# Sparse attention and routed experts on one core: v loaded by one DMA per pair, the last batch transposed by DMA, first weights in quarters

## The chip, the cores and the metric

The kernel runs on one core of one Trainium2 chip, as a single program. Its time is measured on the device, in microseconds (us); the median of nine runs is compared. The profile shows one execution, recorded by the hardware profiler, with its own time and span.

A core has a matrix engine (TensorE, PE in the profile; PEld is its loading of weights), a vector engine (DVE), a scalar engine (ACT), a general engine (POOL, GpSimd) and a queue engine (SP). POOL, SP and ACT also issue DMAs, which the core's 16 DMA engines carry out.

## What is computed

Two stages, one after the other. The first is attention over 4 batches, 8 heads, 768 positions and 64 dimensions, in which each position sees its neighbours nearer than 16 and, besides, a summary of each block of 32 positions:

```python
k_sum = k.reshape(B, H, nb, block, D).max(axis=3)
v_sum = v.reshape(B, H, nb, block, D).mean(axis=3)
scores_l_m = np.where(mask_l, scale * q @ k.T, -1e9)       # |i - j| < 16
scores_s   = scale * q @ k_sum.T + np.log(block)
a = softmax(concatenate([scores_l_m, scores_s]))
attn = a @ concatenate([v, v_sum])
```

Its output, as x with 3072 rows and 512 columns, goes to eight experts, which all work on all rows. Their shares P are found from the logits by eight rounds of normalizing rows and columns (the Sinkhorn rounds):

```python
P = exp(x @ w_gate)
for _ in range(8):
    P /= P.sum(1); P /= P.sum(0); P *= N / E
out = sum(P[:, e] * (relu(x @ w1[e]) @ w2[e]) for e in range(8))
```

## The kernel before

**Pairs and batches.** Heads are worked on two at a time: 16 pairs, four to a batch. Pairs 0 to 3 are done in halves of 384 positions (`pair_half`), pairs 4 to 15 whole (`pair_whole`). For one pair, q and k are loaded by POOL (`load_qk`), turned so that the head dimension lies on partitions (`tr` on TensorE through PSUM, copied out by `tr_out`, line 202, on DVE or ACT), keys are maximized by blocks (`key_max`, lines 315 and 318), scores are formed (`score_mms`, line 324; summaries, line 422), exponentiated on ACT, masked on DVE (`masks`, `edges`), multiplied with v (`values`, lines 410 and 416), normalized on DVE (lines 500 and 501), and turned again into xT (`to_xT`, line 508, with `x_out`). v comes by two DMAs a pair, one per head (`load_v`, line 270). A whole pair also needs the neighbours of each 128-row chunk, which four small SBUF-to-SBUF DMAs on SP put into the tile `Ve` (`near_values`, lines 352 and 354). Sums of v by blocks are line 332.

**Experts.** Expert 0 runs inside this stage in eight halves of 384 rows, two per batch (`expert0`): 32 matmuls of 384 columns (line 206) and 24 of 512 (line 211) each. When the last batch's x is there, its logits (line 528) and the Sinkhorn rounds follow (lines 537 to 551). After it the loop over experts 1 to 7 runs, with 64 matmuls of 512 columns for each of six blocks of rows, and the loads of the next expert (lines 187 and 193). DVE adds each result to `out_acc` (line 867) and SP stores it (line 871).

**What sets the order.** In the first stage the order on every engine is written out by a planner, `Plan.order`, before the kernel is built. Each step is a unit with an engine, a cost in us, its predecessors and a priority. The planner picks the unit that can start first by these costs. The engines then follow that order strictly, so an instruction whose input is late holds up all behind it on its engine. Expert 0 has the lowest priority and fills gaps. Where the planner sees TensorE idle before the first relu, it adds matmuls on a tile of zeros (`keep_busy`, line 570).

**DMA queues.** All loads stand in one chain on POOL (`load`). POOL's DMAs share eight semaphores in turn, so that a DMA waits until the eighth before it has landed. The two loads of expert 1's weights come at the end of the chain, behind `transposed`, two one-element copies on POOL that read kT and qT of pair 12.

Transposing by DMA exists in the code (`tr_dma`, `x_dma`, both issued by SP) but the bounds `BY_DMA = 16` and `X_BY_DMA = 16` keep it out of use: there are only pairs 0 to 15. The planner's own costs for one transposing DMA are 1.4 us on SP (1.5 for x), then 1.7 us, then a lag of 2.0 us.

Of the kernel before, what the change touches and what calls it, by code (L numbers as in the profile page):

```python
# [9 lines left out]
FP32 = mybir.dt.float32  # L10
BF16 = mybir.dt.bfloat16
# [101 lines left out]
def kernel(  # L113
# [10 lines left out]
    nc = tc.nc  # L124
# [18 lines left out]
    NEH = 3  # L143
    BY_DMA = 16
    X_BY_DMA = 16
    WHOLE = 12
# [12 lines left out]
    col_en = const.tile([128, 128], FP32)  # L159
    warm = const.tile([1, 8], FP32)  # L160
    zeros = const.tile([128, 512], BF16)
# [46 lines left out]

    def project_mm(e, yp, h, c, fs):
        for f in fs:  # L210
            nc.tensor.matmul(yp[:], lhsT=h[:, f, c * 128:(c + 1) * 128],  # L211
                             rhs=w2s[e][:, f, :], start=(f == 0), stop=(f == KF - 1))

# [6 lines left out]
    with tc.tile_pool(name="attn", bufs=1) as attn, \  # L220
# [7 lines left out]
        ksT = [attn.tile([128, 128], BF16, name=f"ksT{i}") for i in range(NB)]  # L228
        v_x = [attn.tile([128, G, 2, VD], BF16, name=f"vx{i}") for i in range(NQ)]

# [36 lines left out]
        def load_v(i):  # L267
            b, h0 = i // PB, (i % PB) * 2
            for j in range(2):
                nc.gpsimd.dma_start(out=v_x[i % NQ][:, :, j, 0:D],  # L270
                                    in_=v[b, h0 + j].rearrange("(g p) d -> p g d", p=128))

# [55 lines left out]
        def block_sums(i):  # L328
            sv = v_x[i % NQ]
            vs = at["vs", i] = bank("a", "vs")[:, 0:2 * D]  # L330
            for g in range(G):
                nc.tensor.matmul(vs.rearrange("p (j d) -> p j d", j=2), lhsT=m_blk[:, g, :],  # L332
                                 rhs=sv[:, g, :, 0:D], start=(g == 0), stop=(g == G - 1))

# [11 lines left out]
        def near_values(i):  # L346

            sv, ve = v_x[i % NQ], V_e[i % NE]
            eng = nc.sync if i < BY_DMA else nc.gpsimd
            for j in range(2):  # L350
                c0, q0 = VD * j, 64 + 32 * j
                eng.dma_start(out=ve[q0 + W:q0 + 2 * W, 1:G, c0:c0 + VD],
                              in_=sv[128 - W:128, 0:G - 1, j, :])
                eng.dma_start(out=ve[q0:q0 + W, 0:G - 1, c0:c0 + VD],
                              in_=sv[0:W, 1:G, j, :])

# [47 lines left out]
        def values(i, h):  # L404
            sv, ee, ve, em = v_x[i % NQ], E_e[i % NE], V_e[i % NE], at["em", i]
            av = at["av", i, h] = bank("a", "av")
            for cc in range(HG):
                c, o = HG * h + cc, cc * 2 * VD
                for j in range(2):
                    nc.tensor.matmul(av[:, o + j * VD:o + (j + 1) * VD],  # L410
                                     lhsT=em[:, j, c, :], rhs=sv[:, c, j, :],
                                     start=(cc == 0 and j == 0), stop=False,
                                     skip_group_check=True)
            for cc in range(HG):
                c, o = HG * h + cc, cc * 2 * VD
                nc.tensor.matmul(av[:, o:o + 2 * VD], lhsT=ee[:, c, :], rhs=ve[:, c, :],
                                 start=False, stop=True, skip_group_check=True)
# [46 lines left out]
        def values_h(i, h):  # L464
            sv, em, es = v_x[i % NQ], E_h[(PB * h + i) % NEH], at.pop(("es", i, h))
            av = at["av", i, h] = bank("a", "av")

            def mm(p0, p1, cc, j, lhsT, rhs, n=VD, start=False, stop=False):
                o = cc * 2 * VD + j * VD
                nc.tensor.matmul(av[p0:p1, o:o + n], lhsT=lhsT, rhs=rhs, start=start, stop=stop,  # L470
                                 skip_group_check=True)

            for cc in range(HG):
                for j in range(2):
                    mm(0, 128, cc, j, em[:, j, cc, 2 * W:2 * W + 128], sv[:, HG * h + cc, j, :],
                       start=(cc == 0 and j == 0))
            for cc in range(HG):
                c = HG * h + cc
                for j in range(2):
                    if c + 1 < G:  # L480
                        mm(96, 128, cc, j, em[0:32, j, cc + 1, 0:32], sv[0:32, c + 1, j, :])
                    if c > 0:
                        mm(0, 32, cc, j, em[96:128, j, cc - 1 if cc else HG, LIVE:PADL],
                           sv[96:128, c - 1, j, :])
            for cc in range(HG):
                mm(0, 128, cc, 0, es[:, cc, :], V_s[i][:], n=2 * VD, stop=True)
# [129 lines left out]

        def late_constants():
            for t in E_e:
                nc.vector.memset(t[64:128, :, :], 0.0)
            for t in V_e:  # L620
                nc.vector.memset(t[:], 0.0)
                nc.vector.memset(t[0:24, :, D:VD], 32.0)
                nc.vector.memset(t[32:56, :, VD + D:2 * VD], 32.0)
            nc.vector.memset(col_en, float(E) / float(N))

# [9 lines left out]
        def load_pair(i, parts="kqv"):  # L635
            old = i - NQ
            for c in parts:
                if c == "v":
                    load(("v", i), lambda: load_v(i), 1.65, 1.75,
                         [U.get(("A", old, 1)), U.get(("near", old))])  # L640
                elif i < PB and c in "qr":
                    h = "qr".index(c)
                    load(("q", i, h), lambda h=h: load_qk(i, 1, h), 0.65, 0.6)
                else:
                    z = "kq".index(c)
                    load((c, i), lambda z=z: load_qk(i, z), 0.75 if i < PB else 1.65,
                         1.1 if i < PB else 1.55, [U.get(("tr", old, z)), U.get(("tr", old, 2))])

        def pair_start(i, prio):
# [9 lines left out]
            for z in range(0 if i >= BY_DMA else 1 if i < PB else 2):  # L659
# [9 lines left out]
            U["vs", i] = add("PE", 0.4, lambda: block_sums(i),  # L669
                             [U["v", i]] + ([U.get(("A", i - NE, 1))] if i >= PB else []), prio + 0.01, opens=[buf])  # L670
            U["Vs", i] = add("DVE", 0.22 if i < PB else 0.7, lambda: block_out(i), [U["vs", i]],
# [35 lines left out]
        def pair_whole(i, prio):  # L707
            U["near", i] = add("SP" if i < BY_DMA else "POOL", 2.4 if i < BY_DMA else 3.0, lambda: near_values(i),
                               [U["v", i], U.get(("A", i - NE, 1))], prio, lag=3.5)
            x1 = []  # L710
# [14 lines left out]
            for h in range(2):  # L725
                U["mk", i, h] = add("DVE", 0.56, lambda h=h: masks(i, h),
                                    [U["X", i, h], *x1[:h], U.get(("A", i - 2, 1))], prio)
            U["ed", i] = add("DVE", 0.78, lambda: edges(i),
                             [U["X", i, 0], U["X", i, 1], U["mk", i, 1], U.get(("A", i - NE, 1))], prio)
            for h in range(2):  # L730
# [22 lines left out]
        def expert0(t0, xs):  # L753
            key, n = t0, len(halves)
            halves.append(key)
            pr = 1000.0 + n
            w = [U["w1", 0], U["w1", 1]]
            evac, old = [], [U.get(("pj", halves[n - 2], c)) for c in range(HG)] if n >= 2 else []
            for f in range(KF):
                buf = Buffer("m")  # L760

                def fn(f=f):
                    at["hp", key, f] = hidden0(key, t0, f)
                m = add("PE", 0.67, fn, xs + [w[f // 4]] + old, pr + f * 0.01, opens=[buf])

# [30 lines left out]
        load_pair(3, "v")  # L796
        load(("w1", 0), lambda: load_w1(0, 0, 2), 0.85, 2.5)
        for i in range(PB):
            load_pair(i, "r")
        load(("w1", 1), lambda: load_w1(0, 1, 2), 0.85, 2.5)  # L800
        load("w2", lambda: load_w2(0), 0.85, 5.0)
        add("DVE", 4.0, constants, [], -5.0)
        for i in range(PB):
            pair_start(i, i)
            pair_half(i, 0, i)
        add("DVE", 1.8, late_constants, [U["A", PB - 1, 0]], 5.5)
        expert0(0, [U["x", i, 0] for i in range(PB)])
# [14 lines left out]
        def transposed():  # L822

            r = (NP - 4) % NB
            nc.gpsimd.tensor_copy(out=warm[:, 0:1], in_=kT[r][0:1, 0:1])
            nc.gpsimd.tensor_copy(out=warm[:, 1:2], in_=qT[r][0:1, W:W + 1])

        last[0] = add("POOL", 0.3, transposed, [last[0]] + [U["kT", NP - 4, z] for z in range(2)])
        load("w1n", lambda: load_w1(1), 0.85, 5.0)
# [28 lines left out]
    def step2(e, n):  # L858
        h = hs.pop((e, n))
        for c in range(4):  # L860
            t = 4 * n + c
            if e == 1:
                nc.vector.tensor_scalar_mul(out=out_acc[:, t, :], in0=out_acc[:, t, :],
                                            scalar1=P_sb[:, t, 0:1])
            yp = mps.tile([128, 512], FP32, tag="m", name="yps")
            project_mm(e, yp, h, c, range(KF))
            nc.vector.scalar_tensor_tensor(out=out_acc[:, t, :], in0=yp[:],  # L867
                                           scalar=P_sb[:, t, e:e + 1], in1=out_acc[:, t, :],
                                           op0=ALU.mult, op1=ALU.add)
            if e == E - 1:  # L870
                nc.sync.dma_start(out=out[t * 128:(t + 1) * 128, :], in_=out_acc[:, t, :])

# [35 lines left out]
```

The softmax here doesn't subtract the row's maximum and nothing guards it: scores larger than these inputs give would overflow.

## Time and profile before

| | us |
|---|---|
| median of nine runs | 744.05 |
| lowest and highest of them | 743.80, 746.33 |
| the profiled execution's own time | 745.99 |
| its span in the profile | 744.3 |
| start of expert 1's matmuls in the trace | 159.79 |
| TensorE busy | 730.8 (98%) |
| DVE busy | 373.6 (50%) |
| ACT busy | 201.6 (27%) |
| POOL busy | 90.8 (12%) |

Of the nine runs five lie between 743.80 and 744.05 and four between 745.86 and 746.33; the profiled one belongs to the four.

A line of the profile names the line of the code, the engine, the operation, the tile written and the tiles read (buffer numbers left out), and then how often it ran, how long it was busy and how long its engine stood idle just before it. Matmuls are pipelined, so the busy time shown for one is longer than the spacing between two: a matmul of 512 columns is shown with 379 ns, yet 32 of them start within 6.91 us, one every 0.216 us. Where this text speaks of a pace, it is the spacing of starts. A row of windows shows, for a stretch of time, the busy time of each engine, the TensorE clock granted (1.00 is full), the mean number of busy DMA engines as a share of 16, and the bytes moved.

### The profile page before, as it was taken

The page shows a single profiled execution, that of the slowest core. Times are in us where ns is not written, and L with a number is a line of the kernel's source. Part 1 is how long each engine was busy: PE and PEld are TensorE (multiplying, and loading weights), DVE is VectorE, ACT ScalarE, POOL GpSimd, SP SyncE. Part 2 cuts the span into 40 slices and gives each one's busy share as a digit, 9 for nine tenths or more (in the row PEclk, how much of TensorE's full clock was granted, in tenths as well). Part 3 has the DMA queues.
Part 4 walks back from the last instruction along what each step waited for, and adds up shares of the span by engine and source line. Part 5 has one row for each costly group of instructions (what it writes and reads, how often), then busy time and mean ns, then how long its engine had stood idle before and what let it go on. Part 6 is the DMA issues. An engine that isn't in the chain of part 4 may idle for free.

```text
span 744.3 us, 10242 instructions
## 1 busy us (share of the span) xinstructions
PE 730.8 (98%) x4292; PEld 358.8 (48%) x4364; DVE 373.6 (50%) x734; ACT 201.6 (27%) x343; POOL 90.8 (12%) x118
## 2 busy tenths in 40 slices
PE   7999999999999999999999999999999999999997
PEld 4566666554444444444444444444444444444443
DVE  6789976684444444444444444444444444444443
ACT  4577776442112112112112111111121121121120
POOL 8599700010000000000000000000000000000000
PEclk9999999999999999999999999999999999999999
DMA  9999970051003300123003300212003300001212
GB/s 122 164 129 129 107 119 4 1 84 29 1 1 57 57 1 0 22 38 55 1 1 56 58 1 0 41 27 47 1 1 56 57 1 0 1 1 61 95 71 113
DMA packets 86669, 33.68 MB, mean 45 GB/s; under 512 B 68704, under 2 KB 79968, under 8 KB 86624
## 3 DMA queue, kind: packets, MB, share of 16 engines
q0 software_dynamic: 78032, 26.22, 32.9%
q1 hardware_dynamic: 8064, 6.80, 2.9%
q8 instruction: 34, 0.56, 0.3%
q14 instruction: 11, 0.09, 0.0%
q10 hardware_dynamic: 528, 0.02, 0.0%
HBM read 52.45 MB, written 6.29 MB: 79 GB/s over the span
## 4 chain that ended last, share of the span: by engine, by line
PE 93%; DVE 5%; issue 1%; ACT 0%
PE hps L206 44%; PE yps L211 43%; PE idle L570 1%; DVE xs L501 1%; DVE ks L315 1%; PE sg L324 1%; PE av L470 1%; PE tkq L283 1%; PE tx L508 1%; PE ss L422 1%; DVE em L387 1%; PE vs L332 1%; DVE qT L202 0%; DVE kT L202 0%; DVE Ve L342 0%
## 5 line engine op out<-in xcount | busy, mean ns | idle before, releaser
L206 PE MATMUL hps<-xT,w 128*128 128x512 bf16 (+1 forms) x1574 | 343.3, 370 | 1.4
L211 PE MATMUL yps<-w,h 128*128 128x512 bf16 x1493 | 339.5, 379 | 2.2
L197 ACT ACTIVATE h<-hps 128x512 bf16<-128x512 f32 (+1 forms) x220 | 126.1, 573 | 478.5 <-PE hps L206 461.6
L206 PEld LDWEIGHTS <-w 128*128 128x128 bf16 x1600 | 155.1, 98 | 171.8
L211 PEld LDWEIGHTS <-h 128*128 128x128 bf16 x1536 | 149.9, 98 | 175.6
L867 DVE SCALAR_TENSOR_TENSOR out_acc<-yps,P_sb,out_acc 128x512 f32<-128x512 f32 x168 | 126.1, 751 | 166.4 <-PE yps L211 158.5
L199 DVE TENSOR_SCALAR h<-hps 128x512 bf16<-128x512 f32 (+1 forms) x180 | 122.9, 683 | 169.7 <-PE hps L206 169.4
L187 POOL DMA_DIRECT2D w<-in_moe_w_dram x9 | 7.0, 779 | 372.2 <-PE hps L206 371.8
L270 POOL DMA_DIRECT2D vx<-in_v_dram x32 | 29.4, 1023 | 0.0
L383 ACT ACTIVATE er<-sg 128x960 bf16<-128x960 f32 (+1 forms) x28 | 23.5, 857 | 7.5 <-PE sg L324 3.7
L264 POOL DMA_DIRECT2D kst<-in_k_dram x24 | 22.4, 1048 | 7.5 <-DMA w<-in_moe_w_dram 7.5
L264 POOL DMA_DIRECT2D qst<-in_q_dram x24 | 22.5, 1061 | 0.4 <-DMA qst<-in_q_dram 0.4
L193 POOL DMA_DIRECT2D w<-in_moe_w_dram x8 | 9.0, 1121 | 104.2 <-PE yps L211 104.1
L501 DVE TENSOR_TENSOR xs<-av,rc 128x384 bf16<-128x384 f32 x32 | 17.8, 558 | 1.1
L202 ACT COPY out_acc<-yps 128x512 f32<-128x512 f32 x21 | 12.3, 587 | 17.4 <-PE yps L211 16.9
L315 DVE TENSOR_REDUCE ks<-kT 128x24 bf16<-128x768 bf16 x16 | 15.1, 946 | 0.3
L387 DVE TENSOR_TENSOR em<-er,band 128x768 bf16<-128x768 bf16 x24 | 12.8, 548 | 0.6 <-ACT er L383 0.5
L324 PE MATMUL sg<-qT,kT 64*128 64x160 bf16 x208 | 11.8, 230 | 0.2
L432 ACT ACTIVATE Ee<-ss 64x384 bf16<-64x384 f32 x24 | 11.3, 480 | 1.7 <-PE ss L422 1.6
L422 PE MATMUL ss<-qT,ksT 128*128 128x384 bf16 x32 | 9.9, 330 | 1.0 <-DVE ksT L318 0.8
L570 PE MATMUL idle<-zeros 128*128 128x512 bf16 x25 | 9.3, 498 | 1.5 <-DVE vx L576 1.3
L508 PE MATMUL tx<-ident,xs 128*128 128x128 bf16 x96 | 8.9, 221 | 1.3 <-DVE xs L501 1.2
(92 smaller groups left out, 245.1 us busy)
## 6 DMA issues: line engine op xcount, KB each, us to landing
w<-in_moe_w_dram POOLq DMA_DIRECT2D x15, 1024.0 KB, 8.6
out_dram<-out_acc SPq DMA_DIRECT2D x24, 256.0 KB, 2.0
qst<-in_q_dram POOLq DMA_DIRECT2D x32, 96.0 KB, 4.4
vx<-in_v_dram POOLq DMA_DIRECT2D x32, 96.0 KB, 4.7
kst<-in_k_dram POOLq DMA_DIRECT2D x24, 96.0 KB, 4.5
w<-in_moe_w_dram POOLq DMA_DIRECT2D x2, 512.0 KB, 9.2
kst<-in_k_dram POOLq DMA_DIRECT2D x4, 192.0 KB, 5.1
Ve<-vx SPq DMA_DIRECT2D x48, 10.2 KB, 3.7
```

What stands on the lines that cost most here:

```text
L197: nc.scalar.activation(out=out, in_=in_, func=AF.Relu, bias=0.0, scale=1.0)
L199: nc.vector.tensor_scalar_max(out=out, in0=in_, scalar1=0.0)
L206: nc.tensor.matmul(hp[:, 0:n], lhsT=w1s[e][:, dk, f * 128:(f + 1) * 128], rhs=xT[:, dk, t0:t0 + n], start=(dk == 0), stop=(dk == KD - 1))
L211: nc.tensor.matmul(yp[:], lhsT=h[:, f, c * 128:(c + 1) * 128], rhs=w2s[e][:, f, :], start=(f == 0), stop=(f == KF - 1))
L264: nc.gpsimd.dma_start(out=t[:, :, j, :], in_=src[b, h0 + j].rearrange("(g p) d -> p g d", p=128))
L270: nc.gpsimd.dma_start(out=v_x[i % NQ][:, :, j, 0:D], in_=v[b, h0 + j].rearrange("(g p) d -> p g d", p=128))
L315: nc.vector.tensor_reduce(out=ks[i % 2][:, 0, 0:24], in_=kT[r][:].rearrange("p (n w) -> p n w", w=32), axis=AX.X, op=ALU.max)
L324: nc.tensor.matmul(dst, lhsT=kT[r][p0:p0 + 64, g * 128:(g + 1) * 128], rhs=qT[r][p0:p0 + 64, g * 128 + l0:g * 128 + l1], start=True, stop= ...
L383: nc.scalar.activation(out=dst, in_=src, func=AF.Exp, bias=0.0, scale=SCALE)
L387: nc.vector.tensor_tensor(out=at["em", i][:, :, c, :], in0=at["er", i][:, :, c, W:W + 128], in1=band[:, None, None, W:W + 128].to_broadcas ...
L501: nc.vector.tensor_tensor(out=t.rearrange("p g j d -> p (g j) d"), in0=av[:, :, 0:D], in1=rc[:].to_broadcast([128, G, D]), op=ALU.mult)
L867: nc.vector.scalar_tensor_tensor(out=out_acc[:, t, :], in0=yp[:], scalar=P_sb[:, t, e:e + 1], in1=out_acc[:, t, :], op0=ALU.mult, op1=ALU.add)
```

## The change

Six things change together.

- v of a pair comes by one DMA over both heads in place of two. The tile `vx` has its dimensions swapped for it, and every reader of v is re-indexed.
- `BY_DMA` and `X_BY_DMA` go from 16 to 12: for pairs 12 to 15, q and k are turned by `tr_dma` on SP, and x of pairs 12 to 14 by `x_dma` on SP. x of pair 15 stays on TensorE. By the same bound, `near_values` of pairs 12 to 15 moves from SP to POOL, behind all loads.
- `transposed` now waits for the last pair: it reads kT and qT of pair 15 and two corners of its `Ve`, and its unit follows the near rows of pair 15. So expert 1's weights are loaded behind these.
- w1 of expert 0 comes in four DMAs, two before the second halves of q and two after, and each hidden matmul waits for its own quarter.
- The constants of `late_constants` (1.8 us on DVE in one piece) are cut into four units.
- The last projection of expert 7 is done in two halves of 256 columns, each with its own addition and its own store, the second one issued by ACT.

The planner writes a new order with these units. In it 96 transposes of k and q (line 283) stand on TensorE where there were 144, 78 of x (line 508) where there were 96, and 22 matmuls on zeros where there were 28.

```diff
-    BY_DMA = 16
-    X_BY_DMA = 16
+    BY_DMA = 12
+    X_BY_DMA = 12
...
-        v_x = [attn.tile([128, G, 2, VD], BF16, name=f"vx{i}") for i in range(NQ)]
+        v_x = [attn.tile([128, 2, G, VD], BF16, name=f"vx{i}") for i in range(NQ)]
...
-            for j in range(2):
-                nc.gpsimd.dma_start(out=v_x[i % NQ][:, :, j, 0:D],
-                                    in_=v[b, h0 + j].rearrange("(g p) d -> p g d", p=128))
+            nc.gpsimd.dma_start(
+                out=v_x[i % NQ][:].rearrange("p j g x -> p (j g) x")[:, :, 0:D],
+                in_=v[b, h0:h0 + 2].rearrange("j (g p) d -> p (j g) d", p=128))
...
-                    load(("v", i), lambda: load_v(i), 1.65, 1.75,
+                    load(("v", i), lambda: load_v(i), 0.95, 1.75,
...
-            w = [U["w1", 0], U["w1", 1]]
+            w = [U["w1", n] for n in range(4)]
...
-                m = add("PE", 0.67, fn, xs + [w[f // 4]] + old, pr + f * 0.01, opens=[buf])
+                m = add("PE", 0.67, fn, xs + [w[f // 2]] + old, pr + f * 0.01, opens=[buf])
...
-        load(("w1", 0), lambda: load_w1(0, 0, 2), 0.85, 2.5)
-        for i in range(PB):
-            load_pair(i, "r")
-        load(("w1", 1), lambda: load_w1(0, 1, 2), 0.85, 2.5)
+        for n in range(4):
+            load(("w1", n), lambda n=n: load_w1(0, n, 4), 0.85, 1.25)
+            if n == 1:
+                for i in range(PB):
+                    load_pair(i, "r")
...
-        add("DVE", 1.8, late_constants, [U["A", PB - 1, 0]], 5.5)
+        for n in range(NE):
+            U["ec", n] = add("DVE", 0.42, lambda n=n: edge_constants(n), [U["A", PB - 1, 0]], 15 + n)
+            U["vc", n] = add("DVE", 0.5, lambda n=n: value_constants(n), [U["A", PB - 1, 0]], 15.5 + n)
...
-            r = (NP - 4) % NB
-            nc.gpsimd.tensor_copy(out=warm[:, 0:1], in_=kT[r][0:1, 0:1])
-            nc.gpsimd.tensor_copy(out=warm[:, 1:2], in_=qT[r][0:1, W:W + 1])
-
-        last[0] = add("POOL", 0.3, transposed, [last[0]] + [U["kT", NP - 4, z] for z in range(2)])
+            r = (NP - 1) % NB
+            nc.gpsimd.tensor_copy(out=warm[:, 0:1], in_=kT[r][0:32, 0:1])
+            nc.gpsimd.tensor_copy(out=warm[:, 1:2], in_=qT[r][0:32, W:W + 1])
+            ve = V_e[(NP - 1) % NE]
+            for j in range(2):
+                nc.gpsimd.tensor_copy(out=warm[:, 2 + j:3 + j],
+                                      in_=ve[64 + 32 * j:96 + 32 * j, G - 2, VD * j:VD * j + 1])
+
+        last[0] = add("POOL", 0.3, transposed, [last[0], U["near", NP - 1]] + [U["kT", NP - 1, z] for z in range(2)])
...
-            yp = mps.tile([128, 512], FP32, tag="m", name="yps")
-            project_mm(e, yp, h, c, range(KF))
...
-            if e == E - 1:
-                nc.sync.dma_start(out=out[t * 128:(t + 1) * 128, :], in_=out_acc[:, t, :])
+            parts = 2 if (e, t) == (E - 1, NT - 1) else 1
+            for d0 in range(0, DM, DM // parts):
+                d = slice(d0, d0 + DM // parts)
+                yp = mps.tile([128, 512], FP32, tag="m", name="yps")
+                project_mm(e, yp, h, c, range(KF), d)
+                nc.vector.scalar_tensor_tensor(out=out_acc[:, t, d], in0=yp[:, d],
+                                               scalar=P_sb[:, t, e:e + 1], in1=out_acc[:, t, d],
+                                               op0=ALU.mult, op1=ALU.add)
+                if e == E - 1:
+                    (nc.scalar if d0 else nc.sync).dma_start(out=out[t * 128:(t + 1) * 128, d],
+                                                             in_=out_acc[:, t, d])
```

The functions that the change uses in the last batch and did not before are `tr_dma` (one `dma_start_transpose` of a whole tile of 128x768 two-byte elements, 192 KB) and `x_dma` (the same for x); both stand in the printed functions.

## The prediction

> **What bounds the kernel now.** I read the page first, then busy time by stage, then the chain that ended last, then the matrix engine in order of time, then the DMAs.
>
> ```profile
> PE 730.8 (98%) x4292; PEld 358.8 (48%) x4364; DVE 373.6 (50%) x734; ACT 201.6 (27%) x343; POOL 90.8 (12%) x118
> ```
>
> The share 98% is an average. By stage (columns: stretch, its length, PE, PEld, DVE, ACT and POOL busy with counts, clock, DMA share, GB/s):
>
> ```profile
> 0.00:32.00 32.00, 26.79 (x370) 15.46 (x373) 22.02 (x111) 16.44 (x27) 23.59 (x37) 0.95 1.35 148
> 32.00:96.00 64.00, 63.36 (x765) 42.50 (x771) 57.95 (x153) 46.79 (x78) 55.34 (x69) 1.00 1.82 118
> 96.00:160.00 64.00, 63.34 (x530) 38.01 (x535) 47.08 (x125) 37.26 (x72) 0.88 (x1) 1.00 0.25 41
> 160.00:744.30 584.30, 577.27 (x2634) 262.84 (x2686) 246.59 (x348) 101.08 (x169) 10.95 (x11) 1.00 0.16 32
> ```
>
> Only the first 32 us have gaps on PE. From 32 us on PE is full, with DVE 91% busy beside it until 96. The chain in order of time (start, us, what) says that the end is PE alone:
>
> ```profile
> 155.04 4.91 PE yps L211 x22
> 159.95 5.83 PE hps L206 x27
> ...
> 740.15 0.75 DVE out_acc L867
> ```
>
> From 159.79 to 740.12 stand 2688 matmuls of 512 columns at 0.216 us, with no hole. So the change can only move the start of expert 1 (159.79) and the 4.2 us behind the last matmul. The pace of small matmuls is read from starts on PE:
>
> ```profile
> 57.41 0.50 PE L283 MATMUL tkq<-ident,kst 128*128 128x128 bf16 x6
> 57.74 0.50 PE L283 MATMUL tkq<-ident,qst 128*128 128x128 bf16 x6
> 58.08 0.51 PE L332 MATMUL vs<-vx,m_blk 128*128 128x128 bf16 x6
> ```
>
> Six transposes take 0.33 us of PE, 0.055 each, whatever the 220 ns shown for one. Paces of the other kinds: 0.162 for 384 columns, 0.04 for a score, 0.03 to 0.06 for values. Adding them up along the written order gives 26.9 us at the first transposes of pair 4 (trace: 37.27), 83.0 at pair 12's scores (97.31) and 143.8 at expert 1 (159.79). The lag is 10.4, then 14.3, then 16.0: most of what PE loses, it loses before pair 4. In the changed order the same sums are 25.6, 80.7 and 138.9.
>
> **1. Before pair 4** (v in one DMA, w1 in quarters, six idle matmuls less). One v load has 1536 pieces. POOL rows: 0.81 us for 768 pieces, 0.77 for 512 (w1) and 0.89 for 1024 (w2), so about 1.0 against 1.62 for two; bounds 0.8 and 1.62. That is 0.6 us of POOL per pair, 2.5 before w1. But the DMAs behind POOL are late already. Issues at 20.7 to 23.6 (KB each, median us to landing):
>
> ```profile
> w<-in_moe_w_dram POOLq DMA_DIRECT2D x1, 1024.0 KB, 13.6
> kst<-in_k_dram POOLq DMA_DIRECT2D x2, 96.0 KB, 12.8
> ```
>
> The same kind of load lands 4.2 us after issue at 34.4, so here some 8 us are queueing. Pair 4's k landed at 34.6 and 35.2, with the same bytes ahead of it in the changed kernel. PE came to it at 37.27; with 1.3 us of idle matmuls gone and earlier inputs of pairs 1 to 3 it gets there by about 35, and then waits for the landing. I take 35.2: **-2.1**, bounds 0 (the DMAs decide all) and -3.5 (k lands 1.4 earlier). From pair 5 on POOL's saved time is hidden: PE turns pair 12's k at 91, and it was issued at 68. The constants cut in pieces leave DVE free between 26.2 and 28.7, where they held a mask and PE by 0.4; that too is inside the bound.
>
> The clock bears on this part (columns as above):
>
> ```profile
> 14.00:16.00 2.00, 0.91 (x14) 0.60 (x14) 2.00 (x6) 1.14 (x2) 1.65 (x3) 1.00 2.14 155
> 18.00:20.00 2.00, 1.69 (x16) 1.06 (x18) 2.00 (x4) 1.35 (x3) 1.48 (x3) 0.67 1.26 185
> 20.00:22.00 2.00, 1.78 (x11) 0.77 (x8) 1.08 (x5) 1.00 (x1) 1.59 (x2) 0.50 1.29 177
> ```
>
> PE idled half of 14 to 16, and from 18.7 to about 22.1 ran at half clock, 1.7 us of matmul time; most of it covers waiting for pair 3's v. Escaping it is inside the bound of -3.5. [...]
>
> **2. Transposes off PE.** 48 of k and q and 18 of x, 66 x 0.055 = **-3.6**, all in the stretch where PE is full. The weight loads beside them cost nothing (PEld is 66% busy there). The 11 copies out of PSUM that go as well (nine on DVE at 0.55, two on ACT at 0.8) are not on the path.
>
> **3. DVE.** The changed order packs pairs 4 to 15 into 74 us of PE work where it took 83, and moves one whole half of expert 0 behind pair 15. DVE's durations there sum to 73 us against 78. So DVE is as tight as in 32 to 96, but all the way. There the lag grew 3.9 us per 56; later 1.7 per 61. I take **+0.7**, bounds 0 and 2.
>
> **4. The wait for transposed tiles.** The trace has no transposing DMA. Nearest rows: an SBUF-to-SBUF near row, SP 0.58 us and 3.7 to landing, below; a 96 KB load beside weights, 12.8, above. SP is otherwise idle, and the planner's own 1.4 and 3.7 lie near the lower row; I take them. k and q have room: pair 15's may start after pair 12's scores (sum 81, so about 94 us) and its summaries stand at 106, which leaves 10.4 us for issue and landing once key max (1.2) is off; pair 13 has 10.7 (from 79.3, behind pair 11's near rows on SP, to 90), pair 14 more. Pair 12's stand ahead of pair 11's near rows on SP but may start at 72, when those still wait for pair 9's values (77). Needed: 2.8 + 3.7 = 6.5. Nothing is lost. x of pair 14 has less: its values end at 115.5, normalizing takes 1.3, SP 1.4, so it leaves at about 118, and the logits behind it stand at 123.7, with 19 us of expert 0 queued behind them on PE. It shares the DMAs with expert 1's weights, which leave at about 112.5: pair 13's values end at 105, POOL then issues pair 15's near rows (4 x 0.6 to 0.8), these land, and POOL's copies release the loads. Issues at 90 to 95, near rows beside weights:
>
> ```profile
> w<-in_moe_w_dram POOLq DMA_DIRECT2D x2, 1024.0 KB, 10.6
> Ve<-vx SPq DMA_DIRECT2D x3, 10.2 KB, 7.0
> ```
>
> With 7.0 it lands at 125.0: **+1.3**, bounds 0 (3.7) and 7 (12.8). [...]
>
> The weights themselves leave 19.5 us later than before (93.0), land by 123 and are needed at 156: hidden, with 33 us of cover. The near rows of pairs 12 to 15, now on POOL, follow its last load (about 84) or the values of two pairs before (pair 14's 100, pair 15's 105) and are needed 12 us and more later; a POOL load of 96 KB lands within 4.7. The Sinkhorn rounds are covered by the half of expert 0 moved there.
>
> **5. The end.** DVE at 384 and 512 columns of one kind takes 553 and 692 ns, 1.09 a column, so the last addition falls from 0.75 to 0.47; the store of 128 KB lies between 2.0 us (256 KB) and 1.8 (16 KB). **-0.4**, bounds 0 and -0.8. Sixteen matmuls of 256 columns take what eight of 512 did.
>
> **Sum:** -2.1 - 3.6 + 0.7 + 1.3 - 0.4 = -4.1, expert 1 starting at about 156. The profiled execution took 745.99 (span 744.3 and 1.7 around it) and would take 741.9. It belongs to the upper group of runs; from the median 744.05 the forecast is **740.0**.
>
> **Rivals.**
> - *No early gain.* For: POOL waits for the eighth DMA before, and with quarters w2 becomes the eighth after w1's first quarter, so it can leave only when that has landed, about 22 in place of 19.87. If the DMAs run dry meanwhile, w2 and pair 4's k come as late as now. Against: the other quarters and q are still queued (w1's second half landed at 28.5). Time: 742.1.
> - *x late.* The logits wait 5 to 7 us for pair 14's x behind two weight loads of 1 MB. For: the 12.8 above. Against: those were queued behind the loads on POOL; this is on SP. Time: 743.7 to 745.7, called no change.
> - *Slower: a pair's transposes take over 13.4 us from SP to landing.* Then pair 13's summaries wait (L - 10.7) and, since that shifts pair 12's scores, pair 15's wait again (L - 10.4); at 13.4 the two make up for the 4.1 and 1.5 more. At the upper row, 2.8 + 12.8 = 15.6, this is 4.9 + 5.2 = 10, and the time 750. The order is fixed, so the spare half of expert 0 can't fill it. For: nothing of this kind is in the trace, and POOL's loads keep the DMAs busy until pair 15's are in. Against: near rows land in 3.7 us in that very stretch.
>
> That v in one DMA takes POOL as long as two (1.62) is part of the first rival.
>
> **Numbers.** Forecast 0.53 (736.2 to 741.3: early part and end at their best and nothing lost, or DVE at 2), no early gain 0.15, x late 0.14, slower 0.18. What a measurement of this kernel can tell from no change is about 0.2%, 1.5 us. Faster 0.53 + 0.13 = 0.66 (the first rival can come to rest within 1.5 us); same 0.16; slower 0.18. The range goes from 736.2 to 745.5 and leaves the slower case out.
>
> **What would show it.** Expert 1 starts near 156; 66 transposes less; pair 4's k waits for its DMA near 35; a wait of about 1 us before the logits of batch 3, on DMA, with expert 1's weights in flight; the summaries of pairs 13 and 15 without a wait; the last addition near 0.47. I am wrong if a transposing DMA takes over 7 us, if PE shows more than 2 us of waits on DVE between 36 and 110, or if the first 30 us don't shorten.

## The result and the profile after

The changed kernel takes 738.94 us (median of 10 runs, 738.52 to 741.63) against 744.22 for the kernel before, now over 32 runs. The ratio is 0.9931, with a 95% interval from 0.9921 to 0.9940: 5.3 us less, where 4.1 were forecast. The profiled execution took 739.49, with a span of 737.7.

Of the 45 runs of the kernel before whose mean granted clock is known, 11 show 0.998 or less and take 745.07 to 746.59 (median 745.98), while the other 34 take 743.72 to 744.77 (median 744.24), and the profiled execution of before (0.996) is one of the kind of the 11.

The first line of the page of the changed kernel, and busy time by stage (columns as in the prediction):

```profile
PE 724.8 (98%) x4230; PEld 354.7 (48%) x4300; DVE 368.9 (50%) x728; ACT 198.6 (27%) x339; POOL 95.9 (13%) x122
```

```profile
0.00:32.00 32.00, 27.60 (x409) 16.80 (x413) 24.58 (x118) 18.58 (x30) 23.00 (x36) 1.00 1.39 151
32.00:96.00 64.00, 62.40 (x758) 41.56 (x762) 56.59 (x150) 47.33 (x81) 49.66 (x61) 1.00 2.07 139
96.00:160.00 64.00, 63.28 (x455) 35.38 (x462) 47.28 (x128) 34.00 (x65) 15.04 (x16) 1.00 0.31 50
160.00:737.70 577.70, 571.49 (x2615) 260.93 (x2667) 240.47 (x335) 98.67 (x165) 8.20 (x10) 1.00 0.16 33
```

PE is still the bound. The stretch from 32 to 96 shows 1.6 us without PE where before showed 0.6 (a few matmul records are missing: 758 stand beside 762 weight loads, before 765 beside 771). Two starts on PE cut the run into three parts (start, busy time, then the line):

```profile
33.76 0.50 PE L283 MATMUL tkq<-ident,kst 128*128 128x128 bf16 x6
...
153.94 6.42 PE L206 MATMUL hps<-xT,w 128*128 128x512 bf16 x28
```

| | before, profiled | changed, profiled | difference |
|---|---|---|---|
| start to pair 4's first transposes | 37.27 | 33.76 | -3.51 |
| from there to expert 1 | 122.52 | 120.18 | -2.34 |
| expert 1 to the end of the span | 584.51 | 583.76 | -0.75 |
| span | 744.3 | 737.7 | -6.6 |

The first part of these two executions can't be compared as it stands. The same clock windows as in the prediction, now of the changed kernel, show full clock throughout:

```profile
14.00:16.00 2.00, 1.75 (x48) 1.34 (x45) 1.97 (x6) 1.69 (x2) 1.59 (x3) 1.00 2.31 146
18.00:20.00 2.00, 1.76 (x31) 1.19 (x29) 1.48 (x5) 0.56 (x2) 1.22 (x2) 1.00 1.41 196
20.00:22.00 2.00, 1.81 (x29) 1.12 (x28) 1.55 (x5) 0.48 (x1) 0.89 (x1) 1.00 1.45 188
```

The kernel e4 below has before's order up to the end, and its execution kept the full clock. There pair 4 starts at 35.13:

```profile
35.13 0.50 PE L283 MATMUL tkq<-ident,kst 128*128 128x128 bf16 x6
```

So 2.1 of the 3.51 us lie between two executions of the same order, one with the clock drop and one without; by the medians above the drop is worth about 1.7, and most runs have no such drop.

The middle part can be added up. These are its waits on PE in the changed kernel (in brackets the idle time and what ended it); before had only one, 0.29 at a summary:

```profile
44.79 0.40 PE L416 MATMUL av<-Ve,Ee 128*128 128x130 bf16 x3 [0.36 <-DMA Ve<-vx]
70.89 0.51 PE L508 MATMUL tx<-ident,xs 128*128 128x128 bf16 x6 [0.24 <-DVE xs L501]
82.54 0.34 PE L422 MATMUL ss<-qT,ksT 128*128 128x384 bf16 x1 [0.33 <-DVE ksT L318]
91.42 0.51 PE L508 MATMUL tx<-ident,xs 128*128 128x128 bf16 x6 [0.22 <-DVE xs L501]
105.91 0.34 PE L422 MATMUL ss<-qT,ksT 128*128 128x384 bf16 x1 [0.19 <-DVE xs L501]
...
123.29 1.00 PE L528 MATMUL lp<-wg_bf,xT 128*128 128x8 bf16 x24
```

The logits of batch 3 take 1.00 where they took 0.74: inside the group the fourth tile of x is 0.26 late. Sum: -66 x 0.055 = -3.63 for the transposes, +0.98 - 0.29 = +0.69 for DVE, +0.36 for late near rows of pair 4, +0.26 for x: -2.32, measured -2.34. That is closer than the terms themselves are known: the same sum for e1 below (waits of 0.87 in place of 0.29, nothing else) gives +0.58 where +0.41 was measured.

### The profile page after: what moved, and what is told of

The parts are those of the page before. It is cut to its first block, busy times and chain, and to the rows that moved or that the text cites. A ratio compares the mean times of both kernels' runs of the same rounds, so it can differ in the third digit from the quotient of the medians.

```text
span 737.7 us, 10106 instructions
## 1 busy us (share of the span) xinstructions
PE 724.8 (98%) x4230; PEld 354.7 (48%) x4300; DVE 368.9 (50%) x728; ACT 198.6 (27%) x339; POOL 95.9 (13%) x122
## 4 chain that ended last, share of the span: by engine, by line
PE 88%; DVE 6%; DMA 3%; POOL 2%; issue 1%; SPq 0%; POOLq 0%
PE hps L206 44%; PE yps L211 42%; DVE xs L501 1%; DMA qst<-in_q_dram 1%; DVE ks L315 1%; DMA xT<-xs 1%; DMA Ve<-vx 1%; DVE em L387 1%; PE sg L324 1%; POOL vx L269 1%; DVE Ve L342 0%; POOL kst L258 0%; PE ss L422 0%; DVE rc L500 0%; DVE Ee L399 0%
## 5 line engine op out<-in xcount | busy, mean ns | idle before, releaser
L211 PE MATMUL yps<-w,h 128*128 128x512 bf16 (+1 forms) x1502 | 339.4, 378 | 2.2
L879 DVE SCALAR_TENSOR_TENSOR out_acc<-yps,P_sb,out_acc 128x512 f32<-128x512 f32 (+1 forms) x169 | 126.3, 748 | 166.0 <-PE yps L211 157.9
L187 POOL DMA_DIRECT2D w<-in_moe_w_dram x11 | 15.3, 1393 | 352.0 <-PE hps L206 349.6
L264 POOL DMA_DIRECT2D qst<-in_q_dram x24 | 20.6, 900 | 3.8 <-DMA w<-in_moe_w_dram 3.2
L264 POOL DMA_DIRECT2D kst<-in_k_dram x24 | 20.7, 906 | 0.7 <-DMA w<-in_moe_w_dram 0.7
L193 POOL DMA_DIRECT2D w<-in_moe_w_dram x8 | 7.1, 889 | 100.9 <-PE yps L211 99.8
L202 ACT COPY out_acc<-yps 128x512 f32<-128x512 f32 x24 | 14.1, 586 | 22.7 <-PE yps L211 22.7
L269 POOL DMA_DIRECT2D vx<-in_v_dram x16 | 17.2, 1076 | 0.0
L872 DVE TENSOR_SCALAR out_acc<-out_acc,P_sb 128x512 f32<-128x512 f32 x24 | 9.6, 482 | 0.0
L332 PE MATMUL vs<-vx,m_blk 128*128 128x128 bf16 x96 | 8.1, 219 | 1.4 <-DMA vx<-in_v_dram 1.4
```

The source lines that it names most:

```text
L211: nc.tensor.matmul(yp[:, d], lhsT=h[:, f, c * 128:(c + 1) * 128], rhs=w2s[e][:, f, d], start=(f == 0), stop=(f == KF - 1))
L264: nc.gpsimd.dma_start(out=t[:, :, j, :], in_=src[b, h0 + j].rearrange("(g p) d -> p g d", p=128))
L269: nc.gpsimd.dma_start(out=v_x[i % NQ][:].rearrange("p j g x -> p (j g) x")[:, :, 0:D], in_=v[b, h0:h0 + 2].rearrange("j (g p) d -> p (j g) ...
L879: nc.vector.scalar_tensor_tensor(out=out_acc[:, t, d], in0=yp[:, d], scalar=P_sb[:, t, e:e + 1], in1=out_acc[:, t, d], op0=ALU.mult, op1=A ...
```

## The experiments

"Stretch" is the time from pair 4's first transposes to expert 1's first matmul. It is the steadier measure: e4 and before have the same order there and both show 122.52.

| kernel | median us | ratio to before, 95% interval | pair 4 at | stretch |
|---|---|---|---|---|
| changed | 738.94 | 0.9921 to 0.9940 | 33.76 | 120.18 |
| e1, v alone | 741.74 | 0.9954 to 0.9979 | 32.53 | 122.93 |
| e3, all but the transposing | 741.88 | 0.9964 to 0.9985 | 35.08 | 122.85 |
| e4, last store alone | 743.40 | 0.9987 to 1.0005 | 35.13 | 122.52 |
| e7, e3 with w1 in halves | 741.97 | 0.9945 to 0.9974 | 33.61 | 122.93 |
| e5, plain copies | 738.40 | 0.9896 to 0.9929 | 33.27 | 119.59 |
| e8, e5 with w1 in halves | 738.66 | 0.9901 to 0.9931 | 34.29 | 119.59 |
| f2, e5 with whole constants | 737.90 | 0.9897 to 0.9925 | 32.38 | 119.54 |
| f3, e5 with x on TensorE | 741.12 | 0.9934 to 0.9970 | 36.15 | 120.71 |
| e6, copies in pieces | 741.85 | 0.9938 to 0.9968 | 33.11 | 121.85 |
| f1, finer pieces | 751.40 | 1.008 to 1.012 | 33.51 | 131.84 |
| f4, e1 with POOL delayed | 742.93 | 0.9969 to 0.9995 | 37.05 | 122.94 |

Each ratio is to runs of before taken beside that kernel; their medians go from 744.22 to 744.48. The transposing DMA itself was run in the changed kernel alone; in the experiments plain copies stand in its place, or the transposes stay on TensorE. The kernel before with the transposing DMAs as its only edit has no time.

### v alone, all but the transposing, the last store alone

e1 is the kernel before with the edits of `vx`, `load_v` and its price (0.95). e3 is the changed kernel with

```diff
-    BY_DMA = 12
-    X_BY_DMA = 12
+    BY_DMA = 16
+    X_BY_DMA = 16
```

and the old `transposed`. e4 is the kernel before with the new `project_mm` and the new end of `step2`.

> The kernel before with one edit: v of a pair by one DMA, with vx laid out for it and the planner's price for it (0.95 in place of 1.65). The planner then writes 22 matmuls on zeros where there were 28, as in the changed kernel. Theory: of the 5.3 us by medians, the transposes give about 3.6, the last store about 0.4, and what is before pair 4 about 1.5; the rest of the 3.5 us by which pair 4 came earlier in the profiles was the clock drop of that one execution, which most runs of before do not have. Then this kernel takes 742.7 (744.2 - 1.5), with pair 4's first transposes near 34 and expert 1 near 156 to 158. Rival: the 3.5 us before pair 4 are real and kept, and the transposes by DMA give back half of theirs: 740.7. A second rival: v in one DMA alone does nothing, since quarters of w1 are needed with it: 744.2.

> The changed kernel with its transposes on TensorE again, near rows of the last batch on SP and expert 1's loads where they were before (BY_DMA and X_BY_DMA 16, the old wait). Theory: early part 1.5 and end 0.4 stay: 742.3. Rival (early part 3.5): 740.3. The difference to the changed kernel, 738.9, is what the transposes by DMA are worth inside the whole: 3.4 by the theory, 1.4 by the rival.

> The kernel before with one edit: the last projection in two halves, with two additions and two stores. All theories: 0.4 less, 743.8 (bounds 0 and -0.8), the last addition 0.47 and a store of 128 KB of 1.7 to 1.8 in place of 256 KB. All ahead of the end is the kernel before, so its profile says more: if its clock is full between 18 and 22 us, the theory expects pair 4's first transposes at 35.3 to 35.6 in place of 37.3, and the rival at 37.3 again.

v alone brings 2.5 us, more than the 1.5 of my theory; it lies between theory and rival. e3 brings 2.4, so the transposes by DMA are worth 741.88 - 738.94 = 2.9 inside the whole. That is nearer to the theory (3.4) than to the rival (1.4). e4's ratio is not resolved from 1; in its profile the part from expert 1 on is 583.95, 0.56 shorter than before's, and pair 4 starts at 35.13, near the 35.3 to 35.6 of the theory and not at the rival's 37.3.

That e1 and e3 are alike by time although e3 has e4's end too shows how loose the first part is. It changes from one execution to the next, with nothing different in POOL's order before 11.7 us. In e3's profiled execution (743.60, above its median) PE waits for v, with the clock at 1.00:

```profile
18.43 0.50 PE L332 MATMUL vs<-vx,m_blk 128*128 128x128 bf16 x6 [1.01 <-DMA vx<-in_v_dram]
...
20.34 0.50 PE L332 MATMUL vs<-vx,m_blk 128*128 128x128 bf16 x6 [0.64 <-DMA vx<-in_v_dram]
```

### Quarters and constants

> e3 (all of the change but the transposing DMAs) with w1 of expert 0 in halves again: v in one DMA, the constants in pieces, the last store in halves. Theory: the quarters cost, because two more DMAs stand in POOL's row of eight. In e3 the third quarter left at 18.7 us and w2 at 22.5, where w2 left at 16.9 in e1, and PE waited 2.1 us for v between 13 and 20. Without them this takes e1's 741.7 less 0.5 for the end: 741.2, with pair 4's first transposes near 32.5. Rival: the constants in pieces are what costs e3, or nothing does and e1's start was luck: 741.9 like e3.

> e5 with w1 of expert 0 in halves: what the quarters cost inside the changed kernel. It leaves out the transposing, like e5. Theory: 0.6 less than e5, 738.0, with w2 leaving near 17 us and pair 4's first transposes near 32.5. Rival: the same as e5 (what is gained before pair 4 is lost again while DVE sets the pace between 32 and 96).

> e5 with the constants in one piece of 1.8 us on DVE again, where the kernel before had them. Leaves out the transposing, like e5. From pair 4's first transposes to expert 1 the kernel before and e4 take 122.52 us, e1, e3 and e7 122.85 to 122.93, e5 and e8 119.59. e1 has the constants whole and e7 in pieces, and they are alike. Theory: the constants cost and save nothing: 119.6 for the stretch, 738.4. Rival: with fewer transposes DVE is the tighter engine, and 1.8 us of it in one piece show: 120.1 or more, 738.9.

e7 and e8 take back the edits of w1 (two loads, `w[f // 4]`); f2 puts `late_constants` back. My theory on the quarters fell: with halves e7 takes 741.97 where e3 takes 741.88, and e8 738.66 where e5 takes 738.40. w2 does leave late behind quarters (21.06 in the changed kernel, 16.87 in e1), but in the changed kernel the DMAs moved 183 GB/s between 20 and 26 us, so they had work enough. (In e3's profile, one of its two longest runs, with the same quarters, it was 146, which is what had misled me.) The constants in pieces neither cost nor save in the stretch (119.54 and 119.59). Both edits are worth nothing that these runs can tell.

### What of v's gain is POOL's time

f4 is e1 with a delay behind each v load of pairs 0 to 3:

```diff
                 in_=v[b, h0:h0 + 2].rearrange("j (g p) d -> p (j g) d", p=128))
+            if i < PB:
+                for _ in range(2):
+                    nc.gpsimd.memset(late[:], 0.0)
```

> e1 (v in one DMA, nothing else) with two fills of 128x160 on POOL behind each v load of pairs 0 to 3, about the time that the second DMA took (I take 0.3 us each, from the 0.30 and 0.35 of the two selects of this size). The planner's order on TensorE is e1's, with 22 matmuls on zeros; the row of eight and the number of DMAs are e1's too. Theory: what v in one DMA brings is POOL's time, 0.6 us a pair, because everything behind it on POOL leaves that much earlier: here most of e1's 2.5 us are gone, 743.5 to 744, with pair 4's first transposes near 35. Rival: it is the smaller number of DMAs in the row of eight, or the six matmuls on zeros: 741.7 as in e1.

The two fills took 0.57 us, which with the v load makes 1.62, what the two loads took before. Of its 12 runs four show a granted clock of 0.995 or less and take 745.1 to 746.2; the other eight have a median of 742.7, where e1's five, all at full clock, have 741.74. So POOL's time is worth about 1.0 of the 2.5 us, and neither case was right alone; the ranges of the two kernels meet (741.67 to 743.16 and 741.56 to 741.99), so the 1.0 is rough. The other 1.5 stays with fewer DMAs in POOL's row of eight (in before the k load at 34.44 had waited 4.91 us, by the profile for w2, the eighth DMA ahead of it) and with six matmuls on zeros less (6 x 0.216 = 1.3); which of the two it is, no run here separates. f4's profile is one of the four, and shows what the delay risks. Windows, columns as before:

```profile
14.00:16.00 2.00, 0.83 (x14) 0.58 (x13) 1.68 (x4) 0.77 (x1) 2.00 (x4) 0.96 2.01 160
16.00:18.00 2.00, 0.98 (x16) 0.81 (x17) 0.95 (x4) 0.31 (x2) 1.23 (x3) 0.50 1.86 177
```

PE stood idle for more than half of these 4 us (its longest wait, 1.84, was for pair 3's k) and then had half clock until about 22.7.

### What the transposing DMAs cost

In e5 each `dma_start_transpose` is replaced by a plain copy, and nothing else (shown for q and k; x likewise):

```diff
-            nc.sync.dma_start_transpose(out=dst.rearrange("c (g t) -> c g t", g=G),
-                                        in_=st[:].rearrange("p g j d -> p (g j d)"))
+            nc.sync.dma_start(out=dst, in_=st[:].rearrange("p g j d -> p (g j d)"))
```

f3 has, besides, `X_BY_DMA = 16`.

> The changed kernel in which each of the 11 transposing DMAs is a plain copy of the same tile to the same place, issued by SP in the same order and waited for by the same instructions. What it leaves out is the transposing of q, k and x of the last batch; all else is done. It prices the transposing DMAs themselves: what they cost through their own length, through the loads that share the DMAs with them, and through late tiles. Theory: the changed kernel loses next to nothing to them (its summaries and logits of the last batch show waits of at most 0.3 us), so this takes 738.9 - 0.3 = 738.6. Rival: the 2.9 us between e3 and the changed kernel are less than 66 x 0.055 = 3.6 because the transposing DMAs cost the missing 0.7 us or more (landing 7.5 us for kT where I had 3.7): 738.0 or less.

> e5 with x of the last batch turned on TensorE (18 transposes back, the three x copies gone; q and k as in e5, so their transposing is still left out). Theory: TensorE is full in this stretch, so the 18 transposes cost their pace: 18 x 0.055 = 1.0, less what waiting for DVE fills: stretch 120.3 to 120.6, 739.2 to 739.4. Rival: x by DMA gains nothing, since the logits and the second last half of expert 0 stand where they stood: 119.6 and 738.4.

The landing times between 60 and 125 us, first of the changed kernel (median us from issue), then of e5 (KB each, then us):

```profile
kT<-kst SPq DMA_TRANSPOSE x4, 7.5
qT<-qst SPq DMA_TRANSPOSE x4, 6.6
xT<-xs SPq DMA_TRANSPOSE x3, 3.5
```

```profile
kT<-kst SPq DMA_DIRECT2D x4, 192.0 KB, 4.7
qT<-qst SPq DMA_DIRECT2D x4, 192.0 KB, 3.9
xT<-xs SPq DMA_DIRECT2D x3, 192.0 KB, 2.4
```

A transposing DMA landed 1.1 to 2.8 us later than a plain one of the same tile. That cost little: the stretches differ by 0.59 us (119.59 against 120.18), and 0.36 of that is the wait at pair 4, which no transposing DMA precedes, and 0.26 is x. By medians e5 gains 0.54, and the two intervals overlap.

f3's stretch is 1.12 longer than e5's. 0.18 of that is more waiting for DVE (1.18 in all, against 1.00 in e5); the other 0.94 is what the 18 transposes of x cost when they are back on PE, where 18 x 0.055 = 0.99. Three of its six runs have a granted clock of 0.997 or less, which is why its median lies at 741.12; the other three take 739.43 to 739.91, near the 739.2 to 739.4 expected.

### How late the tiles may be

e6 cuts each copy of q and k into 3072 pieces, f1 into 6144 (e6's edit is shown; f1 has 16 and 0:15 in place of 32 and 0:31):

```diff
-            nc.sync.dma_start(out=dst, in_=st[:].rearrange("p g j d -> p (g j d)"))
+            nc.sync.dma_start(out=dst.rearrange("c (n w) -> c n w", w=32)[:, :, 0:31],
+                              in_=st[:].rearrange("p g j d -> p (g j d)").rearrange("p (n w) -> p n w", w=32)[:, :, 0:31])
```

> As e5, but each copy of q and k is cut into 3072 pieces of 62 bytes (the last two bytes of every 64 are left out), so that it lands late. It leaves out the transposing, too. From the early part (some 11000 packets in 24 us with all DMAs busy) 3072 pieces need about 7 us, so that k and q of a pair take about 15 us from SP to landing. The forecast's slower case had 10.7 and 10.4 us of room for pairs 13 and 15, and a wait of L less the room in each: at 15 it expects about 4.3 + 4.6 us more than e5, some 747.5. Theory from the profile of the changed kernel: SP issued pair 15's k at 87.7, not at 94, because nothing in the data holds it back, so pair 15 has some 16 us and waits for nothing; only pair 12 (11.5 of room) and 13 (10.1) can be late, and what they lose is lost once: 738.6 + 5 = 743.6. A third case: loads of pairs 14 and 15 queue behind the pieces, and the time goes beyond 750.

> As e6, with pieces of 30 bytes (6144 a tile; the last two bytes of every 32 are left out, and the transposing). In e6 k and q of pair 12 held SP from 72.2 to 83.4, so that pair 11's near rows behind them came 6 us late and TensorE waited 1.95 us; the tiles of pairs 13 to 15 followed at 2.1 us each and were waited for by nobody. Theory: the price of slow transposes is set on SP, by the near rows queued behind pair 12's. Twice as long, they leave at about 95 where TensorE wants them at 85 to 86, some 10 us, and the tiles of pair 15 (six at 4.2 us from 95) come at about 125 where they are wanted at 105 + 10: 10 more. 738.4 + 15 to 20 = 753 to 758. Rival, the forecast's sum with L about 22 to 25 a pair: 11 to 14 for pair 13 and as much for pair 15, 761 to 767, with the waits at the summaries of these pairs and none at the near rows.

Both came in below all cases: e6 at 741.85 (743.6 and 747.5 expected), f1 at 751.4 (753 to 758, and 761 to 767). In e6 PE waits once, at the first summary of pair 12; in f1 there and at the first summary of pair 13. First e6, then f1:

```profile
87.39 0.32 PE L422 MATMUL ss<-qT,ksT 128*128 128x384 bf16 x1 [1.95 <-DVE Ee L395]
```

```profile
89.97 0.48 PE L422 MATMUL ss<-qT,ksT 128*128 128x384 bf16 x1 [4.69 <-DMA qT<-qst]
...
101.67 0.48 PE L422 MATMUL ss<-qT,ksT 128*128 128x384 bf16 x1 [4.11 <-DMA qT<-qst]
```

The name in e6's bracket misleads. Its qT of pair 12 was issued at 73.03 and took 14.2 us, so it landed at 87.2, 0.16 before the summary; the name is that of a DVE step that happened to end late as well. The summary does not need that step: in the changed kernel it runs at 85.70, and the step only at 87.19. So the wait is the forecast's slower case, and my theory for f1, that the near rows behind the tiles set the price, fell. (For e6 I had named pair 12, with 11.5 us of room, and pair 13; only pair 12 waited.) What the forecast's case had wrong is the place. Pair 12 has the least room: SP starts it at 72.1 to 72.2 and PE could have summarized at 85.3 to 85.4, 13.2 us. e6 needed 15.0 and f1 17.7, and the waits follow one for one (1.95 and 4.69). Pair 13 waits in f1 because SP, full with pair 12, began it only at 90.24; pair 15 never waits.

f1's two waits sum to 8.8, but its stretch is 12.25 longer than e5's. The other 3.45 go with the clock, here at the first wait:

```profile
86.00:88.00 2.00, 0.00 (x0) 0.00 (x0) 1.95 (x6) 0.00 (x0) 0.00 (x0) 0.95 1.35 36
88.00:90.00 2.00, 0.03 (x1) 0.06 (x2) 0.62 (x4) 0.00 (x0) 0.00 (x0) 0.50 0.17 13
```

It fell 2.5 us after PE went idle, and PE worked on at half clock behind both waits (0.48 for a summary in place of 0.33), until about 94.6 and 104.8. That is 7.8 us at half clock, so by an estimate 3.9 lost, near the 3.45. With it f1 is 1.0% slower than before. f1's waits are of 4.69 and 4.11 us; f4's drop came in a stretch whose longest wait is 1.84, and before's in one with none over 1.05. At what idle time the clock falls, these runs do not show.

In the changed kernel pair 12's tiles leave SP like this:

```profile
72.95 1.52 SPq L310 DMA_TRANSPOSE kT<-kst  x1
74.59 1.44 SPq L310 DMA_TRANSPOSE qT<-qst  x1
```

This qT took 9.7 us and landed at 84.3; the summary stands at 85.70. The change has 1.4 us to spare there: from SP's start at 72.95 it needs 11.3 of 12.75 us.

## Why the prediction was right, and where it was not

**Sum.** -4.1 was forecast, -5.3 came. By its terms: start -2.1, measured about -2.2 (see 1.); middle -3.6 + 0.7 + 1.3 = -1.6, measured -2.34; end -0.4, measured -0.75.

**1. Before pair 4.** The size holds by luck, and the reason does not hold. By medians what is left for the start is 5.3 - 2.34 - 0.75 = 2.2; two executions at full clock (e4 and the changed kernel) differ by 1.4, and the eight other profiles with v in one DMA and full clock up to there start pair 4 between 32.38 and 35.08. Two things were wrong. The -2.1 was read from 37.27, in an execution with the clock drop, and then taken off a median whose runs mostly have none: in e4, without the drop, before's order comes to pair 4 at 35.13, so the forecast's own 35.2 would have left nothing to gain. And the step said that PE would come to pair 4 and wait for k, because the same bytes stood ahead of it. PE did not wait: k landed at 32.2 to 32.8, not at 34.6 to 35.2. The change did not bring that alone, for in e4 k landed at 32.5 and 32.95, more than 2 us before PE came to it. How soon the same bytes move differs between executions. Packets from 2 to 26 us in before, e4, the changed kernel, e1 and e3, in this order:

```profile
DMA packets 10119, 3.59 MB, mean 150 GB/s; under 512 B 6918, under 2 KB 10116, under 8 KB 10116
DMA packets 10194, 3.67 MB, mean 153 GB/s; under 512 B 6917, under 2 KB 10191, under 8 KB 10191
DMA packets 11329, 3.81 MB, mean 159 GB/s; under 512 B 6896, under 2 KB 11326, under 8 KB 11326
DMA packets 10472, 4.00 MB, mean 167 GB/s; under 512 B 6869, under 2 KB 10469, under 8 KB 10469
DMA packets 11110, 3.58 MB, mean 149 GB/s; under 512 B 6915, under 2 KB 11107, under 8 KB 11107
```

e3 has v in one DMA and moved as little as before, so these rows don't show that one DMA moves the bytes sooner. What v in one DMA is worth stands on the times (e1: 2.5), and POOL's part of it on f4: about 1.0. v in one DMA took 1.03 us on POOL (1.0 forecast). Escaping the clock drop was put inside the bound; it is worth about 1.7 in the runs that have it.

**2. Transposes.** 66 x 0.055 = 3.63. e5's stretch is 3.3 shorter than e3's and e7's, with 0.1 more of waits for DVE in it, so the 66 give about 3.4, and by f3 18 of them give 0.94 (0.99 by the pace). Right to a tenth.

**3. DVE.** +0.7 forecast, +0.69 measured, in four short waits. The size is right, but not the cause: e1 has three such waits of 0.87 in all with every transpose still on PE, so at least these come with v's edit and the order that it brings, not with the transposes that left.

**4. The wait for transposed tiles.** The term that was mis-sized: +1.3, measured +0.26. Landing was right by the row that I took: pair 14's x took 6.9 us beside expert 1's weights (7.0 taken). But SP issued it at 116.68, not at 118, so it landed at 123.6, when the logits had just begun. For k and q I had 3.7 and found 4.5 to 9.7. Nothing was lost, but with 1.4 us to spare where the forecast saw several. The forecast also held pair 15's tiles back until pair 12's scores; that is the planner's bookkeeping and no wait of the hardware, and SP issued the first of them at 87.7, where pair 12's scores stand at 93.9. One of the signs named as "wrong if" came (a transposing DMA over 7 us) and did not decide, because the room from issue to first use, 12.75 us for pair 12, is what counts.

**5. The end.** The last addition, 0.47 forecast:

```profile
734.32 0.48 DVE L879 SCALAR_TENSOR_TENSOR out_acc<-yps,P_sb,out_acc 128x256 f32<-128x256 f32 x1 [0.39 <-PE yps L211]
```

Right, and the halved store gives the rest: the part from expert 1 on is 0.75 shorter in the changed kernel and 0.56 in e4, within the bounds of 0 and 0.8.

**Rivals.** No early gain: w2 left at 21.06, as that rival said (22), but the DMAs did not run dry. x late: 0.26 in place of 5 to 7. Slower: real, as f1 shows with plain copies in pieces; waits begin where pair 12 needs more than about 13 us (e6 needed 15.0 and was still faster than before, f1 17.7); the changed kernel needed 11.3.

Not settled: how v's remaining 1.5 us divide, and whether the changed kernel without quarters and pieces is any better. The plain-copy kernels show no cost of taking them back one at a time (738.40 with both, 738.66 and 737.90), but no run has the transposing DMA without them.

## What to carry to other kernels

Where one engine is full, as PE is here, work moved off it pays its pace (66 transposes: 3.63 us by the pace, about 3.4 measured), and the sum comes near if every new wait of some tenths is listed; look at the room from issue to first use for each tile, not at whether a DMA is fast (pair 12 lost nothing with 11.3 us needed, and waited 1.95 and 4.69 with 15.0 and 17.7). Compare a start that hangs on DMAs only between executions with the same granted clock, and expect it to move by a microsecond or two anyway (32.38 to 35.08 at full clock here); a gain read from an execution with a clock drop may not be taken off a median of runs without one. The name in a wait's bracket is a guess: hold it against the landing time of every other input before building on it.

## What was not expected of the hardware

- The granted clock fell at short gaps, and not in each execution: 11 of 45 runs of the same kernel before show 0.998 or less. In f4 it fell at about 15.9, at the end of 2 us in which PE was busy for 0.83, with no wait over 1.84 us; in before at 18.7, 2.7 us behind a stretch of 2 us in which it was busy for 0.91, with no wait over 1.05; it stayed up in e3, where PE was busy 1.27 of each 2 us from 16 to 20 and the longest wait was 1.01.
- A transposing DMA of 128x768 two-byte elements held SP for 1.2 to 2.6 us in the changed kernel, a plain copy of the same tile mostly for 0.5 in e5, and it landed in 2.9 us at best (x), 9.7 at worst (pair 12's q, beside loads in small pieces: 9077 of the 9078 packets from 74.5 to 84.3 us are under 512 B).
- SP stalled behind slow copies: with 3072 pieces a tile (e6), the issue of one near row behind them took 6.0 us on SP, where most others took 0.6.
